# How the last block's results are stored: the first part in column halves, the last part as one 128 KB store per queue

## The chip, the cores and the metric

The kernel runs on one core of one Trainium2 chip. The time is device time in microseconds (us) of one execution; smaller is better. Of the kernel before there are three timed runs (median 608.53 us) and one profiled execution, whose trace all readings below come from.

Engines are named as the profile names them: PE is the matrix engine (its weight loads are PEld), DVE the vector engine, ACT the scalar engine, POOL the general one, SP the engine that mostly issues transfers. A "q" behind a name (SPq, ACTq) means the engine's instruction sequencer, which also issues DMA transfers. DMA transfers are carried out by 16 DMA engines that all queues share.

## The reference

Two stages follow each other. The first is a chunked state-space scan (Mamba-2) over 4 sequences, 8 heads, 768 steps and 32 channels per head, with a state of 16; its output is viewed as 3072 tokens of 256 numbers. The second is a mixture of four experts, all used for every token:

```
p = domain_probs / (domain_probs.sum(-1, keepdims=True) + 1e-09)
for e in range(E):                      # E = 4
    h = np.maximum(x @ w1[e], 0.0)      # (3072, 256) @ (256, 1024)
    out += p[:, e:e + 1] * (h @ w2[e])  # (3072, 1024) @ (1024, 256)
```

Everything is in 32-bit floats. The output is 3072 rows of 256 numbers, 1 KB per row.

## The kernel before, in words

The second stage takes nearly all of the time. The 3072 tokens are 12 pairs of 256 tokens (`NP` = 12), and three pairs form a block (`BLOCKS` = 4). A block is passed over the 16 column blocks of the hidden layer (four experts, four blocks of 256 columns each) in units of four. In each unit the matrix products are done by a fast scheme (`G`): 20 block products in place of 24, paid for by sums and differences on DVE and POOL before and after. The results of the products add up in accumulators, which lie in PSUM banks while PE writes them and otherwise in SBUF tiles called V (`[128, 2, 256]`). At a block's end some 20 additions combine its accumulators into the outputs of the block's three pairs, which the kernel numbers n = 0, 1, 2 and which this text calls parts.

For all blocks but the last this is done under cover of the next block's products (`result`, `leave`). The last block has nothing behind it, so it is ended by a function of its own, `last`. In it each part is turned by PE and copied from PSUM to an SBUF tile whose partition holds tokens and whose free dimensions are s (two sequence halves) and m (the 256 output columns). The work goes by pieces: `piece(d, n, ...)` makes the sum for column half d of part n, lets PE turn both s (two transposes, L1422) and copies the result out (L1435). The pieces come in the order (d=0, n=1), (1, 1), (1, 0), (0, 0), (1, 2). The last piece, column half 0 of part 2, is made differently: its two PSUM banks (`ends`, one for each s, here i) are filled with the turned partial sum, and the last products are added into them (L1498). So the last instruction that computes anything is the copy of s = 1 out of its bank; ACT copies s = 0 and DVE s = 1.

Part n of the block is stored by `send` (L1427). A partition index of the SBUF tile is 64 c + i, with c = 0 or 1, and the output is viewed as follows, so that a step in c is a step of 12 x 64 rows in DRAM:

```
dst = out.rearrange("(s c n i) m -> n c i s m", s=2, c=2, i=HALF)
```

`send` issues one transfer for each c, c = 0 on SP's queue and c = 1 on ACT's, each from 64 partitions. Parts 1 and 0 go as two stores of 128 KB when both column halves are copied; part 2 goes as two stores of 64 KB for each s.

The order of the instructions is not that of the code. Every piece of work is handed to a planner (`Plan.add`), with estimated times for each engine, the values that it reads and writes, and the works that it must follow. `Plan.run` lets all engines advance in planned time. PE's order is fixed beforehand (`line`; `TAILS` puts the transposes among the last products), every other engine takes, of the works that are ready, the one with the earliest due time (`latest`, reckoned back from the end). The engines then get their instructions in the order of planned starts. Three rules of the planner matter here:

```
        for v in part:
            w.needs.update(v.readers)
            v.writers = v.writers + [w]
```

A work that writes a part of a value must follow all works so far that read the value, whatever part of it they read. For a transfer (`kb` set) planned time goes on until its data has landed: it takes `ISSUE` = 0.55 us to issue, 1.4 us more to start, its kilobytes at `RATE` = 330 per us, and 0.7 us. And a work on another engine than SP that follows a transfer is planned `MARGIN` = 2.0 us after the landing.

Of the kernel before, what the change touches and what calls it, by code (L numbers as in the profile page):

```python
# [12 lines left out]
P = 128  # L13
# [7 lines left out]
LANDING = 2.2  # L21
# [9 lines left out]
LANES, ISSUE = 8, .55  # L31
# [328 lines left out]
def kernel(  # L360
# [10 lines left out]
    nc = tc.nc  # L371
# [14 lines left out]
    HALF = P // 2  # L386
# [352 lines left out]
    for x in range(4):  # L739
# [3 lines left out]
        out=a_sb, in_=a.rearrange("c h s -> (c h) s").rearrange("(p r) s -> p r s", r=2))  # L743
    load_w1(1, homes["W"][1])
    nc.sync.dma_start(
        out=homes["gate"][0][:, :2].rearrange("p c s -> p (c s)"),
        in_=p_d[:1, 0].rearrange("x z i -> x (z i)").partition_broadcast(P))
# [38 lines left out]
    for s, copy in enumerate((nc.scalar.copy, nc.vector.tensor_copy)):  # L786
        copy(out=yT0[:, :, P * s:P * s + P].rearrange("p t (c i) -> p c t i", c=2),
             in_=ys[s][:, :FB].rearrange("p (c t i) -> p c t i", c=2, t=NT))
# [7 lines left out]
    for s in range(2):  # L796
        v = bound[HALF * s:HALF * s + HALF]
        nc.gpsimd.affine_select(
            out=v, in_=v, compare_op=ALU.is_ge, fill=0.0, base=0, pattern=[[1, HALF]],
# [4 lines left out]
    plan = Plan(homes)  # L804
# [18 lines left out]
    def value(kind, **kw):  # L823
        return Value(kind, **kw)
# [186 lines left out]
    def flat(v):  # L1011
        return v.t.rearrange("p a m -> p (a m)")
# [12 lines left out]
    def whole(v):  # L1025
        return v.t if v.kind == "bank" else flat(v)
# [298 lines left out]
    def terms_of(key, groups, house, put={}):  # L1325

        return [(acc, weights[key, fbs, 2][0][r],
                 lambda r=r, fbs=fbs: weights[key, fbs, 2][1](r), T[r])
                for acc in house for r in put.get(acc, acc) for fbs, T in groups if r in T]

    def second(k, key, groups, houses, held=(), put={}):

        seq = []
        for house in houses:
            terms = terms_of(key, groups, house, put)
            if terms:
                seq += visit(k, house, terms, house in held)
        return seq
# [9 lines left out]
    def sum_(x, y, sign, o):  # L1348

        vs = dict.fromkeys((x[0], y[0]))  # L1350
        engines = B256 if all(v.kind != "bank" for v in (*vs, o[0])) else {"DVE": D256}
        plan.add(engines, lambda e: (on(e).tensor_add if sign > 0 else on(e).tensor_sub)(  # L1352
            o[1](), x[1](), y[1]()), reads=[v for v in vs if v is not o[0]],
            two=all(v.kind != "bank" for v in vs), writes=[o[0]])

    def accumulators(k, houses):

        def acc(house, i):
            v = kept[k, house]
            return v, lambda: whole(v)[:, i * FB:i * FB + FB]  # L1360

        return {r[0]: acc(h, i) for h in houses for i, r in enumerate(h)}
# [44 lines left out]
    def last(k, groups):  # L1407

        seq = second(k, k, groups, LATE, HELD)
        A = accumulators(k, LATE)  # L1410
        dst = out.rearrange("(s c n i) m -> n c i s m", s=2, c=2, i=HALF)
        tails, last_of = [], (0, 1)

        def fresh():
            v = value("V")
            return v, lambda: v.t[:, 0]

        def into(r, x, y, sign=1):
            sum_(A[x], A[y], sign, A[r])

        def turn(o, t, i, at):
            nc.tensor.transpose(t.t[:, at:at + P], o[1]()[:, i * P:i * P + P], ident)  # L1422

        def send(n, r, to):
            by = ((nc.sync, "SP"), (nc.scalar, "ACT"))
            for c, (queue, on_) in enumerate(by):
                plan.add({on_: ISSUE}, lambda e, c=c, queue=queue: queue.dma_start(  # L1427
                    out=dst[3 * k + n, c][:, to], in_=r.t[HALF * c:HALF * c + HALF, to]),
                    lag=LANDING + .4, kb=64 * (to.stop - to.start), reads=[r], port=False)

        ready = [[value("V")] * 2 for _ in range(2)] + [[value("V") for _ in range(2)]]

        def copied(x, r, t, d, n, to):
            copy = (nc.vector.tensor_copy, nc.scalar.copy)[x]
            plan.add({("DVE", "ACT")[x]: .1 + .13 * (to.stop - to.start)}, lambda e: copy(  # L1435
                out=r.t[:, to, d * P:d * P + P],
                in_=t.t[:, :P * (to.stop - to.start)].rearrange("p (s m) -> p s m", m=P)),
                reads=[t], part=[r])

        def piece(d, n, x, y, sign):  # L1440
            o, rs = fresh(), ready[n]
            ts = [value("bank", fills=False) for _ in dict.fromkeys(rs)]
            sum_(x, y, sign, o)
            tails.append(plan.add({"PE": .35}, lambda e: [
                turn(o, ts[i % len(ts)], i, i * P if len(ts) == 1 else 0) for i in range(2)],
                reads=[o[0]], writes=ts))
            x = len(tails) % 2
            if len(ts) == 1:
                copied(x, rs[0], ts[0], d, n, slice(0, 2))
                if d == last_of[n]:  # L1450
                    send(n, rs[0], slice(0, 2))
            else:
                for i in range(2):
                    copied(0, rs[i], ts[i], d, n, slice(i, i + 1))

        into(9, 9, 10)
        into(7, 7, 9)
        into(7, 7, 15)
        into(15, 15, 13)
        into(9, 9, 11, -1)  # L1460
        into(11, 11, 7, -1)
        q = A["q"] = fresh()
        sum_(A[11], A[13], -1, q)
        into(13, 13, 7)
        into(10, 10, 15)
        into(4, 4, 8)
        into(4, 4, 9)
        into(8, "q", 8, -1)
        into(15, 15, 4)
        piece(0, 1, A[1], A[11], -1)  # L1470
        piece(1, 1, A[5], A[4], 1)
        into(15, 15, 12)
        into(15, 15, 14)
        into(8, 8, 14, -1)
        piece(1, 0, A[16], A[15], -1)
        into(8, 8, 16)
        piece(0, 0, A[0], A[8], 1)

        into(10, 10, 12)
        into(10, 10, 14)  # L1480
        two, three = APART
        terms = terms_of(k, groups, APART)
        begun = kept[k, APART]
        seq += visit(k, APART, terms, True, three)
        third = kept[k, (three,)]
        piece(1, 2, (third, lambda: whole(third)[:, FB:]), A[10], 1)
        o, ends = fresh(), [value("bank", seeded=True) for _ in range(2)]
        sum_((begun, lambda: flat(begun)[:, :FB]), A[13], 1, o)
        tails.extend(plan.add({"PE": .2}, lambda e, t=t, i=i: turn(o, t, i, 0), reads=[o[0]], writes=[t])
                     for i, t in enumerate(ends))  # L1490
        for i, t in enumerate(ends):
            for acc, w, view, x in terms:
                if acc != two:
                    continue

                def fn(e, i=i, t=t, view=view, x=x):
                    for j in range(JJ):
                        nc.tensor.matmul(  # L1498
                            out=t.t[:, :P], lhsT=x.t[:, j, i * P:i * P + P], rhs=view()[:, j],
                            start=False, stop=j == JJ - 1, skip_group_check=True)  # L1500

                seq.append(plan.add({"PE": .52}, fn, reads=[w, x], writes=[t]))
            copied(1 - i, ready[2][i], t, 0, 2, slice(i, i + 1))
            send(2, ready[2][i], slice(i, i + 1))
        return [w for i, x in enumerate(seq)
                for w in (*[t for t, n in zip(tails, TAILS) if n == len(seq) - i], x)]

# [51 lines left out]
    for seq, _ in plain[EARLY:]:  # L1559
# [10 lines left out]
        out=g0.t[:, 2:].rearrange("p c s -> p (c s)"), in_=p_d.rearrange(  # L1570
            "(x a) e z i -> x (a e z i)", x=E)[0, 2 * P:6 * P].partition_broadcast(P)),
        kb=256, reads=[pd], part=[g0])
# [61 lines left out]
    for u, (k, fbs) in enumerate(units):  # L1634
        of_block = [v for v, (q, _) in enumerate(units) if q == k]
        i = u - of_block[0] + (not k)
# [13 lines left out]
        final = u == len(units) - 1  # L1650
        groups = [(fbs, fours_right(h))]
        behind = last(k, groups) if final else second(k, k, groups, G.houses)
        if u == of_block[-1] and k < len(blocks) - 1:
            ending = k, result(k)
# [25 lines left out]
    for w in done:  # L1680
        n = len(traced)
# [52 lines left out]
```

## Time and profile before

| what | value |
|---|---|
| timed runs | 608.45, 608.53, 608.77 us; median 608.53 |
| the profiled execution: own time, span from first to last instruction | 607.16 us, 605.5 us |
| PE busy | 599.2 us, 99% of the span |
| DVE, ACT, POOL busy | 499.6, 277.3, 135.0 us |
| granted clock of PE | 1.000 all through |
| last product and last copy (DVE) end | 601.3 and 601.6 us into the span |
| last store issued, last store landed | 602.0 and 604.25 us into the span |

The page of the profile gives busy times, shares and the costliest groups of instructions; the other views used are the order of time (timeline), who waited for whom, stretches (windows), and the DMA view, which shows in 40 slices of a stretch which share of the 16 DMA engines was busy, in tenths. For single packets and for the steps in which a transfer reports its landing, the records of the trace are used directly: each DMA engine that took part in a transfer reports once, by a write of 4 bytes.

### The profile page before, as it was taken

To read this page: it belongs to the slowest core of one execution; us is meant where nothing else is said; L and a number is where in the kernel's file an instruction comes from. 1 tells how busy PE (TensorE), PEld (TensorE's weight loads), DVE (VectorE), ACT (ScalarE), POOL (GpSimd) and SP (SyncE) were. 2 spreads that over 40 slices of the span, in tenths; PEclk is the share of its full clock that TensorE was granted. 3 is DMA by queue.
4 is the path that set the end of the run, shared out by engine and by line. 5 is a ranking of instruction groups with operands and counts; after the bars stand their busy time and mean duration, and the time that the engine had idled before them with its cause. 6 is when DMAs were issued, how large, how long until landed. Compare 5 with 4: busy or idle time off the path is not lost.

```text
span 605.5 us, 12443 instructions
## 1 busy us (share of the span) xinstructions
PE 599.2 (99%) x4616; PEld 516.3 (85%) x4616; DVE 499.6 (83%) x867; ACT 277.3 (46%) x621; POOL 135.0 (22%) x147
## 2 busy tenths in 40 slices
PE   9999999999999999999999999999999999999997
PEld 6778888888888888888888888888888888888886
DVE  7879999999999995897979988486876989485795
ACT  3456476783443527764242343434444242444530
POOL 7652836656510000465201000000000000000000
PEclk9999999999999999999999999999999999999999
DMA  5786858779625229763422425963242332964001
GB/s 177 222 220 202 252 172 287 222 230 300 219 79 143 55 47 359 232 202 134 139 88 62 144 33 162 291 178 110 87 132 69 97 74 50 364 183 139 0 1 53
DMA packets 100196, 93.98 MB, mean 155 GB/s; under 512 B 34480, under 2 KB 69416, under 8 KB 100136
## 3 DMA queue, kind: packets, MB, share of 16 engines
q1 hardware_dynamic: 99444, 92.70, 50.8%
q8 instruction: 36, 0.59, 0.4%
q10 hardware_dynamic: 628, 0.47, 0.2%
q14 instruction: 24, 0.20, 0.1%
q0 software_dynamic: 64, 0.02, 0.0%
HBM read 72.89 MB, written 20.27 MB: 154 GB/s over the span
## 4 chain that ended last, share of the span: by engine, by line
PE 98%; DVE 2%; ACT 0%; issue 0%
PE bank L1007 91%; PE bank L535 2%; PE bank L502 1%; PE bank L940 1%; PE bank L544 1%; PE bank L690 1%; PE bank L644 1%; DVE v L1053 0%; DVE v L1042 0%; PE bank L1498 0%; DVE MT L510 0%; PE bank L1422 0%; PE bank L659 0%; DVE v L1034 0%; DVE MT L687 0%; ACT v L1052 0%
## 5 line engine op out<-in xcount | busy, mean ns | idle before, releaser
L1007 PE MATMUL bank<-v,w 128*128 128x256 f32 x1876 | 435.3, 380 | 0.8 <-DVE v L1042 0.4
L1007 PEld LDWEIGHTS bank<-v,w 128*128 128x128 f32 x1876 | 354.6, 190 | 52.2 <-DVE v L1042 1.4
L1034 DVE TENSOR_TENSOR v<-v,v 128x512 f32<-128x512 f32 x239 | 176.0, 757 | 3.1 <-ACT v L1016 1.2
L1007 PE MATMUL bank<-Y,w 128*128 128x256 f32 x692 | 177.2, 380 | 0.1
L1316 ACT COPY v<-bank 128x512 f32<-128x512 f32 x120 | 70.3, 586 | 199.5 <-PE bank L1007 199.3
L1007 PEld LDWEIGHTS bank<-Y,w 128*128 128x128 f32 x692 | 130.6, 190 | 19.6 <-ACT v L1016 0.9
L1042 DVE SCALAR_TENSOR_TENSOR v<-bank,gate 128x512 f32<-128x512 f32 x158 | 108.3, 686 | 36.1 <-PE bank L1007 32.4
L1076 POOL TENSOR_TENSOR w<-w,w 128x512 f32<-128x512 f32 (+1 forms) x81 | 90.1, 1122 | 98.0 <-DMA xt<-in_xbc_dram 30.9
L1174 DVE TENSOR_TENSOR bank<-bank,v 128x512 f32<-128x512 f32 x92 | 63.8, 695 | 34.1 <-PE bank L1007 22.9
L1016 ACT COPY v<-bank 128x512 f32<-128x512 f32 x111 | 65.1, 587 | 55.1 <-PE bank L1007 46.2
L1021 ACT COPY bank<-v 128x512 f32<-128x512 f32 x141 | 81.4, 592 | 19.2 <-DVE v L1042 15.6
L518 ACT ACTIVATE MT<-ab,neg 128x64 f32<-128x64 f32 x144 | 37.4, 338 | 0.0
L1034 DVE TENSOR_TENSOR v<-bank,v 128x512 f32<-128x512 f32 x30 | 20.6, 687 | 8.8 <-PE bank L1007 8.2
L1352 DVE TENSOR_TENSOR v<-v,v 128x256 f32<-128x256 f32 x65 | 24.5, 422 | 1.1 <-ACT v L1316 0.9
L902 POOL TENSOR_TENSOR cts<-ctm,dec 128x512 f32<-128x512 f32 x11 | 14.3, 1301 | 40.3 <-DVE v L1034 30.3
L1042 DVE SCALAR_TENSOR_TENSOR v<-v,gate 128x512 f32<-128x512 f32 x30 | 21.6, 719 | 0.4
L959 ACT COPY v<-bank 64x256 f32<-64x256 f32 (+1 forms) x33 | 12.3, 373 | 19.3 <-PE bank L544 16.2
L1034 POOL TENSOR_TENSOR v<-v,v 128x512 f32<-128x512 f32 x11 | 14.0, 1273 | 20.9 <-DVE v L1034 14.0
L687 DVE TENSOR_TENSOR MT<-bank,MT 128x256 f32<-128x256 f32 x47 | 16.7, 415 | 0.2
L523 DVE TENSOR_TENSOR MT<-MT,bound 128x512 f32<-128x512 f32 x18 | 16.0, 895 | 0.7 <-ACT MT L518 0.7
L490 ACT ACTIVATE ctm<-bct,tmask 128x256 f32<-128x256 f32 (+1 forms) x26 | 11.0, 484 | 8.0 <-DMA bct<-in_xbc_dram 4.0
L535 PEld LDWEIGHTS bank<-MT,xt 64*32 64x32 f32 x768 | 9.1, 105 | 2.6 <-issue 1.8
(94 smaller groups left out, 194.0 us busy)
## 6 DMA issues: line engine op xcount, KB each, us to landing
w<-w_d SPq DMA_DIRECT2D x128, 256.0 KB
w<-in_w_dram SPq DMA_DIRECT2D x72, 256.0 KB
w_d<-w SPq DMA_DIRECT2D x64, 256.0 KB
gate<-p_d SPq DMA_DIRECT2D x15, 384.0 KB
xt<-in_xbc_dram SPq DMA_DIRECT2D x48, 96.0 KB
ab<-cum_d SPq DMA_DIRECT2D x36, 128.0 KB
bct<-in_xbc_dram SPq DMA_DIRECT2D x5, 512.0 KB
out_dram<-v SPq DMA_DIRECT2D x144, 16.0 KB
```

The source lines that it names most:

```text
L518: nc.scalar.activation(out=MT[:, q, c, t], in_=ab[:, c, h], func=AF.Exp, bias=neg[:, e, t, i:i + 1])
L535: nc.tensor.matmul(out=y[to:to + 32], lhsT=xt[k, c, h:h + D], rhs=MT[k, q, c, t], start=start, stop=True, tile_position=(HALF * s, to), sk ...
L687: nc.vector.tensor_mul(v, bank[:, FB * half:FB * half + FB], v)
L1007: nc.tensor.matmul(out=o, lhsT=w[:, j], rhs=x if half is None else x[:, j], start=(start and j == 0), stop=(j == 1), skip_group_check=True)
L1016: act(.5, lambda e: nc.scalar.copy(out=flat(v), in_=bank.t), reads=[bank], writes=[v])
L1021: act(.54 if to - lo > FB else .32, lambda e: nc.scalar.copy(out=bank.t[:, lo:to], in_=flat(v)[:, lo:to]), reads=[v], writes=[bank])
L1034: plan.add(engines, lambda e: (on(e).tensor_add if sign > 0 else on(e).tensor_sub)(flat(v), whole(x), whole(y)), reads=[x, y], writes=[v], ...
L1042: dve(D512, lambda e: nc.vector.scalar_tensor_tensor(out=h.t, in0=whole(x).rearrange("p (j m) -> p j m", j=JJ), scalar=0.0, in1=g.t[:, 2 * ...
L1076: (on(e).tensor_add if sign > 0 else on(e).tensor_sub)(out, x, y)
L1174: dve(D512, lambda e: (nc.vector.tensor_add if sign > 0 else nc.vector.tensor_sub)(to.t, bank.t, whole(x)), reads=[x, bank], writes=[to])
L1316: act(.5, lambda e: nc.scalar.copy(out=flat(v), in_=bank.t), reads=[bank], writes=[v], hold=HOLD)
L1352: plan.add(engines, lambda e: (on(e).tensor_add if sign > 0 else on(e).tensor_sub)(o[1](), x[1](), y[1]()), reads=[v for v in vs if v is n ...
```

## The change

Two things change in `last`.

Part 0 is stored by column halves: after the piece (1, 0), its column half d = 1 is sent (two stores of 64 KB, one on each queue, 128 runs of 512 bytes each), and after the piece (0, 0) the half d = 0 in the same way. Part 1 goes as before.

Part 2 is stored by `send_half`: for each s, one store of 128 KB from all 128 partitions, s = 0 on SP's queue and s = 1 on ACT's. The DRAM side of this store has the sizes (c, i, m) = (2, 64, 256), the SBUF side (128, 256). The number of store instructions stays eight, four on each queue.

```diff
-        def send(n, r, to):
-            by = ((nc.sync, "SP"), (nc.scalar, "ACT"))
-            for c, (queue, on_) in enumerate(by):
-                plan.add({on_: ISSUE}, lambda e, c=c, queue=queue: queue.dma_start(
-                    out=dst[3 * k + n, c][:, to], in_=r.t[HALF * c:HALF * c + HALF, to]),
-                    lag=LANDING + .4, kb=64 * (to.stop - to.start), reads=[r], port=False)
+        queues = {"SP": nc.sync, "ACT": nc.scalar}
+
+        def send(n, r, ds=slice(0, 2)):
+            m, size = slice(P * ds.start, P * ds.stop), ds.stop - ds.start
+            for c, on_ in enumerate(queues):
+                plan.add({on_: ISSUE}, lambda e, c=c, on_=on_: queues[on_].dma_start(
+                    out=dst[3 * k + n, c][:, :, m], in_=r.t[HALF * c:HALF * c + HALF, :, m]),
+                    lag=LANDING + .4, kb=64 * size, reads=[r], port=False)
+
+        def send_half(n, r, i, on_):
+            plan.add({on_: ISSUE}, lambda e: queues[on_].dma_start(
+                out=dst[3 * k + n][:, :, i], in_=r.t[:, i]),
+                lag=LANDING + .4, kb=128, reads=[r], port=False)
...
                 copied(x, rs[0], ts[0], d, n, slice(0, 2))
-                if d == last_of[n]:
-                    send(n, rs[0], slice(0, 2))
+                if n == 0:
+                    send(n, rs[0], slice(d, d + 1))
+                elif d == last_of[n]:
+                    send(n, rs[0])
...
             copied(1 - i, ready[2][i], t, 0, 2, slice(i, i + 1))
-            send(2, ready[2][i], slice(i, i + 1))
+            send_half(2, ready[2][i], i, ("SP", "ACT")[i])
```

## The prediction

> **What bounds the kernel now.** First the page: busy times and the chain that ended last.
>
> ```profile
> span 605.5 us, 12443 instructions
> PE 599.2 (99%) x4616; PEld 516.3 (85%) x4616; DVE 499.6 (83%) x867; ACT 277.3 (46%) x621; POOL 135.0 (22%) x147
> ...
> PE 98%; DVE 2%; ACT 0%; issue 0%
> ```
>
> PE fills the span up to about 601.3. The change touches nothing that PE waits for, so only the few microseconds behind PE can move. The order of time over the end shows them (start, duration, engine, line, what):
>
> ```profile
> 598.87 0.37 ACT L1435 COPY v<-bank 128x256 f32<-128x256 f32 x1 [3.47 <-PE bank L1422]
> 599.84 0.98 DVE L1435 COPY v<-bank 128x256 f32<-128x256 f32 x3 [0.64 <-PE bank L1422]
> 600.22 0.27 ACT L1435 COPY v<-bank 128x128 f32<-128x128 f32 x1 [0.97 <-PE bank L1498]
> 600.24 1.06 PE L1498 MATMUL bank<-w,v 128*128 128x128 f32 x8
> 600.29 2.29 ACTq L1427 DMA_DIRECT2D out_dram<-v  x3
> 601.33 0.29 DVE L1435 COPY v<-bank 128x128 f32<-128x128 f32 x1 [0.51 <-PE bank L1498]
> ```
>
> ACT's copy at 598.87 is piece (1, 0). DVE's three from 599.84 are piece (0, 0), 128x256, and the two of piece (1, 2), 128x128, at 600.33 and 600.53. The last copy (s = 1) ends at 601.62. After that there are only stores: SP issues its last at 601.75; ACT its own at 601.96, because its issue before (601.05, 0.81 us) has only just ended. Then the waits of SP, with total, times and longest:
>
> ```profile
> SPq L1730 <- DMA out_dram<-v: 1.9, 1, 1.9
> ```
>
> SP closes the program once all stores have landed: the last report of a landing is at 604.25, the span ends 1.25 later. Issue to last landing is 2.33 us on SP (604.08) and 2.29 on ACT. Last, the DMA view, once from 601 to 605.5 and once from 173.9 to 176.4, where little but the loads of `ah` (128 partitions of 256 bytes each) runs:
>
> ```profile
> DMA  0000049899979999987699840000000000000000
> ...
> DMA  0155620000015552000001666300000134432910
> ...
> ah<-cumh_d SPq DMA_DIRECT2D x2, 32.0 KB
> ```
>
> The closing stores use nine tenths of the 16 DMA engines, though they are small. An `ah` load alone, between idle slices, stays at five to six tenths, or eight engines; its packet records hold 8 completion writes of 4 bytes where a closing store's hold 16. Its SBUF side has 128 partitions, its DRAM side is (8, 16, 64). The start of the kernel has two more such rows: loads whose slowest dimension is 4 report landings from 4 engines, stores of 24 partitions from 12. All of these fit one reading: the engines are as many as divide the slowest dimension of both sides, 16 at most.
>
> **The change, part by part.**
>
> *Part 2 as one store per queue.* It takes two of the four last stores away. What that saves: ACT's last issue need not wait for another one, so it starts at 601.70 in place of 601.96 (-0.2 us). But the new store's DRAM side is (2, 64, 256): its slowest dimension is c, whose step is 12 x 64 rows, so that it can't be merged with i. By the reading above 2 engines carry it, 64 packets of 1 KB each, where a 64 KB store now gives 4 packets to each of 16. No row shows two engines; the price of a packet is there: 46 ns is the median of all 6,264 packets of 1 KB, and the 16 packets that an `ah` load gives each engine run back to back (16 x 18 = 0.29 us of a burst of 0.30 to 0.39). So 64 x 46 = 2.94 us for one store alone.
>
> SP's store (s = 0) needs the copies that end at 600.49 and 600.62; its queue is free, so it issues at about 600.70. From issue to a first packet it takes 1.29 (600.29 to 601.58) to 1.34 us: 602.0. ACT's store (s = 1) issues at 601.70, first packet 603.05; SP's is then a third through. Do they share the two engines? Bounds: apart, ACT's ends at 603.05 + 2.94 = 606.0 at the earliest; on the same two, 128 packets take 5.89 from 602.0, to 607.9. I take the same two: over the 36 `ah` loads after 23 us, issued four in a row, more than 12 packets overlap for 0.05 us in all, where 2 KB loads on 16 engines overlap up to 21; if each load took the next eight engines, overlapping loads would fill 16. That row is of one queue only, so both ends stay.
>
> The Trainium skill, page "DMA: Bandwidth & Descriptors", section "Why a DMA increments its semaphore by 16 and not by 1", says that such a transfer gets the largest count up to 16 that divides the slowest dimension of both sides, and on SP's and ACT's queues the lowest-numbered engines. By that rule both stores sit on the same two engines, and the sum is the one for 607.9; the trace agrees on the count (8, 4, 12), and no run here shows which engines.
>
> *Part 0 in halves.* One more issue on each queue. The half d = 1 is ready at 599.24, issues at 599.30 on both and is through by 599.95 (0.64), at worst 600.11 (0.81): before ACT's copy at 600.22, so this costs nothing; without that cover ACT's copy, and SP's store behind it, would be late by the excess. Its packets (512 bytes, 27 ns median, 8 per engine per store) come at 600.6 to 601.6, before part 2's. The half d = 0 does not go earlier. In the planner its copy writes part of the value that the first half's stores read, so it must follow them: they land 0.55 + 1.4 + 2 x 64/330 + 0.7 = 3.04 us after the copy of (1, 0), plus a margin of 2.0. From 599.24 that is 604.3 in the trace's time, and the last copy is planned for 601.33. So DVE's order turns round: the two copies of (1, 2), the last copy, then the copy of (0, 0), 128x256, 0.42 us, from about 601.6 to 602.05. Nothing is queued behind it on DVE, and its bank is wanted by none. If the program also makes it wait for the landing of the half d = 1 (599.30 + 2.54 to 2.90, by the 128 KB stores at 600.29), it runs to 602.2 to 602.65. Its two stores then issue last: SP at 602.1, and ACT behind its part 2 store at 602.4 (up to 602.7). On 14 engines they land by about 605; on the pair they add 2 x 8 x 27 ns = 0.43 us.
>
> *Due times.* Sums for piece (1, 0) become due about 2 us sooner, which may swap additions on DVE between 586 and 599. DVE idles 0.66 us before 593.03 and 0.37 before 596.93 waiting for PE, and PE's order is fixed: 0, bounds -0.3 to +0.3.
>
> *Sum.* Pair busy from 602.0 for 5.89 + 0.43: 608.3. Last packet to last landing is now 0.35 to 0.54 (599.13 to 599.48, 603.71 to 604.25): 608.75 in place of 604.25, +4.5 us. The span becomes 610.0 against 605.5, the profiled execution 611.7 against its own 607.16 (1.66 outside the span). The median stands 1.37 above that execution; the difference added to it gives 613.0.
>
> The packet's price may be higher with two queues on one engine: in 601 to 605 SP's packets have a mean of 63.3 ns and ACT's 50.4, and SP's at 597.9, with ACT's behind them, 79.5. At the mean of the first two, 57, the pair takes 1.4 more (614.4), at 79 4.2 more (617.2). Such a packet's time may hold waiting beside the other queue's packet on the same engine, while the engine moves data all along; so I stay with 46.
>
> **The rivals.**
>
> *Two pairs of engines* (both queues pick differently): SP's done by 605.2, ACT's by 606.4 with the halves, landed 606.9: +2.6, 611.1. For it: no row of two queues. Against: the `ah` row.
>
> *Sixteen engines after all* (not slower than can be told): the store is spread as by its 128 partitions. Then 128 KB give 8 packets per engine and only the turned order counts. ACT's store of the half d = 0 issues at 602.4 to 602.7 and lands 2.3 to 2.5 later: 604.7 to 605.2, +0.45 to +0.95, so 609.0 to 609.5. It decides from the point where an engine gets so few packets that the half d = 0 lands last: with four engines part 2 still ends at 605.8 (64 x 46 ns = 2.94 from 602.0, 0.43, 0.4), with eight it does not. Against it: `ah` has the same 128 partitions and got 8.
>
> *The change does what it says*: sixteen engines and the copy of (0, 0) in its old place. Part 1's two stores, issued together at 596.58, landed at 599.15 and 599.48, so a second half-store trails by 0.33; with one store fewer behind each other the end comes near 604.1: 608.4. The Trainium skill, same page, section "Rules for kernel authors", advises exactly this: one 128-partition transfer in place of two on partition halves, since these share the engines; the trace agrees that they trail each other (0.33 us). By that rule alone the time would be 608.4. Against: the count of engines, and the planner's rule.
>
> **How the numbers follow.** A measurement of this kernel can tell some 0.2% (1.2 us) from no change: under 607.3 is faster, over 609.75 slower. Chances: same pair at 46 to 57 ns, 0.67 (612.7 to 614.4, its own range); same pair and dearer packets, 0.08 (to 617.2); two pairs, 0.13 (611.1); sixteen engines with turned order, 0.09; as it says, 0.02; faster for a reason I don't see, 0.01. Slower therefore 0.88, same 0.11, faster 0.01. The range takes the first and third whole and half of the second: 610.6 to 615.8.
>
> **What would show it.** In the DMA view after 602, a long stretch at one tenth where now nine tenths stand for two microseconds; landing reports of part 2's stores from 2 engines; SP's closing wait near 6 us. DVE's last copy of L1435 is 128x256, after the 128x128 ones, and its stores are issued last on both queues. PE's last matmul ends at 601.3 within 0.3. The prediction is wrong if part 2's stores report from 16 engines, if packets on the pair take far from 46 ns, or if PE's end moves.

## The result, and the profile after

The changed kernel takes 613.54 us (median of 6 runs, 612.09 to 614.54) against 608.49 us (6 runs, 607.74 to 608.77): a ratio of 1.0087, 95% interval 1.0074 to 1.0101. That is 5.05 us more; forecast were 4.5, 613.0 us.

The profiled execution has a span of 612.0 us. Its page:

```profile
span 612.0 us, 12443 instructions
PE 599.0 (98%) x4616; PEld 515.8 (84%) x4616; DVE 502.2 (82%) x867; ACT 277.5 (45%) x621; POOL 134.3 (22%) x147
```

PE has the same work and its share is lower: something was added around it. The order of time over the end (start, duration, engine, line, what; PE's rows left out):

```profile
600.85 0.64 ACTq L1429 DMA_DIRECT2D out_dram<-v  x1
601.80 0.27 ACT L1442 COPY v<-bank 128x128 f32<-128x128 f32 x1 [0.98 <-PE bank L1507]
601.91 0.49 DVE L1442 COPY v<-bank 128x128 f32<-128x128 f32 x2 [1.13 <-PE bank L1422]
602.27 0.58 SPq L1434 DMA_DIRECT2D out_dram<-v  x1
602.91 0.62 DVE L1442 COPY v<-bank 128x128 f32<-128x128 f32 x2 [0.51 <-PE bank L1507]
603.24 0.59 ACTq L1434 DMA_DIRECT2D out_dram<-v  x1
603.57 0.62 SPq L1429 DMA_DIRECT2D out_dram<-v  x1
603.93 0.61 ACTq L1429 DMA_DIRECT2D out_dram<-v  x1
```

The copy of s = 1, the last one that waits for a product of PE, starts at 602.91 where it started at 601.33. The row at 602.91 holds two copies: the second, from 603.12, is the 128x256 one of piece (0, 0), which was the first of DVE's copies before. Its two stores are the last to be issued. Behind them SP waits for 6.5 us:

```profile
SPq L1739 <- DMA out_dram<-v: 6.5, 1, 6.5
```

The DMA view of the stretch from 602.9 to the end (slices of 0.23 us) shows what for:

```profile
DMA  0001111122023468941111110111111110000000
```

Before, the closing stores filled nine tenths of the DMA engines for two microseconds. Now there is one short peak, with some two microseconds at one or two tenths ahead of it and three and a half at one tenth behind it. The landing records say who works there: each of part 2's stores reports from two engines, s = 0 at 4.35 us after the start of the copy of s = 1, s = 1 at 7.74. The last of all is ACT's store of part 0's half d = 0: fourteen of its reports come by 4.6, the last two only at 7.94 and 7.95, when the two engines of s = 1 are free. These two engines are called the **pair** below, as in the prediction.

A measure that leaves the rest of the kernel out is used from here on, the **tail**: from the start of DVE's copy of s = 1 to the end of the span. It was 4.13 us (601.33 to 605.46, the span unrounded; 4.17 in the expectations below, from the rounded one) and is 9.09, so +4.96. What is left of the difference between the two profiled spans, 1.59 us, is upstream: PE is 1.06 us late at 14 us into the span, 0.70 at 20 and 1.47 by 33, and stays within 0.3 of that to the end. On DVE, ACT, POOL and SP both kernels have the same instructions in the same order up to this end; PE's records differ from each other only in the order of some small products and weight loads, nearly all in the first 11 us, as they do between the runs below too. This lateness comes and goes from run to run: PE's last matmul ended between 601.1 and 603.5 us in the profiled executions below, 601.1 in one with the changed kernel's order. It is hardly in the medians: the execution profiled before was 1.33 us under its median, the one after 0.18 over its own.

### The profile page after: what moved, and what is told of

It is laid out like the page before. It is cut to its first block, busy times and chain, and to the rows that moved or that the text cites. A ratio compares the mean times of both kernels' runs of the same rounds, so it can differ in the third digit from the quotient of the medians.

```text
span 612.0 us, 12443 instructions
## 1 busy us (share of the span) xinstructions
PE 599.0 (98%) x4616; PEld 515.8 (84%) x4616; DVE 502.2 (82%) x867; ACT 277.5 (45%) x621; POOL 134.3 (22%) x147
## 4 chain that ended last, share of the span: by engine, by line
PE 94%; DVE 2%; DMA 1%; issue 1%; SPq 0%; ACT 0%; DVEq 0%; POOL 0%; POOLq 0%
PE bank L1007 90%; PE bank L535 1%; PE bank L940 1%; PE bank L502 1%; DMA w<-in_w_dram 1%; DVE v L1042 1%; PE bank L544 1%; DMA v<-in_a_dram 0%; PE bank L1507 0%; SPq L471 0%; DVE MT L523 0%; PE bank L1422 0%; DVE v L1034 0%; DVE MT L687 0%; DVE MT L510 0%
```

## The experiments

### Part 2 stored as before

Part 2 goes back to its four stores of 64 KB, called **quarters** from here on:

```diff
         def send_half(n, r, i, on_):
-            plan.add({on_: ISSUE}, lambda e: queues[on_].dma_start(
-                out=dst[3 * k + n][:, :, i], in_=r.t[:, i]),
-                lag=LANDING + .4, kb=128, reads=[r], port=False)
+            for c, on_ in enumerate(queues):
+                plan.add({on_: ISSUE}, lambda e, c=c, on_=on_: queues[on_].dma_start(
+                    out=dst[3 * k + n, c][:, i], in_=r.t[HALF * c:HALF * c + HALF, i]),
+                    lag=LANDING + .4, kb=64, reads=[r], port=False)
```

> The changed kernel with part 2 stored as before (four stores of 64 KB), part 0 still in column halves. The measure is the tail: from the start of DVE's copy of s = 1 (128x128, the last one that PE's products wait on) to the end of the span; 4.17 us before (601.33 to 605.5), 9.09 after the change (602.91 to 612.0). Theory 1 (two engines carry part 2's stores): the tail falls to 4.6 to 5.1, what is left over 4.17 being the turned order (copy of (0, 0) last); time 609.0 to 609.5. Rival 2 (the turned order and the half stores of part 0 cost the time): the tail stays at 8.5 to 9.1, time 613.

Measured: 608.86 us against 608.11, ratio 1.0015 (1.0004 to 1.0026); tail 4.85. The tail is as theory 1 had it; the time is 0.14 us under its range, and the kernel before took 0.38 less in these runs than in those above. The DVE order is still turned:

```profile
602.41 0.62 DVE L1443 COPY v<-bank 128x128 f32<-128x128 f32 x2 [0.52 <-PE bank L1508]
```

So taking part 2's stores back removes 4.24 of the 4.96 us, and the rest of the change by itself costs 0.72.

### Part 0 stored whole

```diff
-                if n == 0:
-                    send(n, rs[0], slice(d, d + 1))
-                elif d == last_of[n]:
+                if d == last_of[n]:
                     send(n, rs[0])
```

> The changed kernel with part 0 stored whole as before, part 2 still as one 128 KB store per queue. Theory 1 (two engines): nearly all of the loss stays; the pair carries 128 packets of 1 KB at 46 to 54 ns and no 512-byte ones, so the tail is 7.9 to 8.9, time 612.3 to 613.3. Rival 2 (turned order, halves): tail back at 4.2, time 608.5. Rival 3 (the halves of part 0 block the pair beside part 2's stores): tail 6.5 to 7.5.

Measured: 613.4 us, ratio 1.0087 (1.007 to 1.0103); tail 9.60. Theory 1 named the cause, but its size was wrong: without the halves and the turned order the tail is not shorter but 0.51 longer, so the two parts of the change do not simply add up. Two things differ in the records. SP's store of s = 0 is issued 0.29 us before the start of the last copy instead of 0.65, since the whole store of part 0 stands ahead of it on the queue; and the pair still carries its share of part 0's packets then, whose last reports come 1.50 (SP) and 2.01 us (ACT) after that start. One of the two engines reports 0.86 us after the other for both of part 2's stores (5.23 and 6.09, 7.56 and 8.42), where they report together after the change. Why one lags was not settled.

### Part 0's halves in two tiles

On top of the first experiment, so that the planner has no reader of the tile ahead of the second copy:

```diff
+        apart = [value("V") for _ in range(2)]
...
-                copied(x, rs[0], ts[0], d, n, slice(0, 2))
+                r = apart[d] if n == 0 else rs[0]
+                copied(x, r, ts[0], d, n, slice(0, 2))
                 if n == 0:
-                    send(n, rs[0], slice(d, d + 1))
+                    send(n, r, slice(d, d + 1))
```

> As the run with part 2 stored as before, but the two column halves of part 0 lie in two tiles, so that the planner sees no reader of the first half ahead of the second copy. Theory: the copy of (0, 0) goes back before those of (1, 2) on DVE and the tail is 4.0 to 4.3, time 608.3 to 608.6: the turned order was all that the first half of the change cost. Rival: the half stores of part 0 cost something by themselves (two more issues, 512-byte packets): tail 4.5 to 5.0.

Measured: 607.56 us, ratio 0.9993 (0.9983 to 1.0003); tail 3.80. DVE's order is the old one:

```profile
601.50 0.98 DVE L1445 COPY v<-bank 128x256 f32<-128x256 f32 x3 [0.64 <-PE bank L1422]
602.99 0.29 DVE L1445 COPY v<-bank 128x128 f32<-128x128 f32 x1 [0.51 <-PE bank L1511]
```

The order alone is 4.85 - 3.80 = 1.05 us. The halves without it save 0.33 of the tail against before, which puts it 0.2 under the range expected; the time can't tell that from nothing.

### The number of engines, with nothing else changed

Part 2's two stores keep their size, source and queue and go to a DRAM tensor aside, whose slowest dimension is A = 2, 4 or 8 with gaps, or 128 rows in one piece (there the tile is 128 x 256 and written whole). These kernels leave part 2's rows of the output unwritten:

```diff
+        aside = [tc.dram_tile([A, 2, 128 // A, 2 * P], FP32, name=f"aside{i}") for i in range(2)]
...
-                out=dst[3 * k + n][:, :, i], in_=r.t[:, i]),
+                out=aside[i][:, 0], in_=r.t[:, i]),
```

> The changed kernel, but part 2's two stores of 128 KB go to a DRAM tensor aside, so that its 704 of 768 output rows per quarter stay as they are and part 2's are left unwritten. The DRAM side is (2, 64, 256) with a gap between the two, as in the output: a control. Theory 1 (the engine count is what divides the slowest dimension of both sides): tail 8.8 to 9.3 as after the change (9.09), landing reports from 2 engines. Rival 2 (something of the output tensor's rows, or DRAM pages 768 KB apart): the tail falls clearly, below 8.

> The same with a DRAM side of (4, 32, 256) with gaps; part 2's output rows are left unwritten. Theory 1: reports from 4 engines; 2 x 32 packets of 1 KB each and the halves' 16 of 512 bytes, from 0.6 us after the copy's start at 46 to 55 ns: 3.0 to 3.9 us; tail 5.2 to 6.2. Rival 2 (one 128-partition store on the DRAM side of several pieces is slow whatever their number): 9.

> The same with a DRAM side of (8, 16, 256) with gaps; part 2's output rows are left unwritten. Theory 1: reports from 8 engines, 2 x 16 packets each, 1.5 to 2.2 us; the turned order decides now: tail 4.6 to 5.2. Rival 2: 9.

> The same with a DRAM side of 128 rows in one piece; part 2's output rows are left unwritten. Theory 1: reports from 16 engines, tail 4.5 to 5.1, that is the price of the turned order alone, 0.4 to 0.9 over before. Rival 2: 9.

Measured, in us; landings count from the start of the copy of s = 1. These four kernels, and the four below them, ran once each:

| slowest dimension in DRAM | engines that report | s = 0 landed | s = 1 landed | part 0's last half landed | tail |
|---|---|---|---|---|---|
| 2 | 2 | 4.35 | 7.81 | 8.01 | 9.15 |
| 4 | 4 | 2.70 | 6.25 | 6.46 | 7.60 |
| 8 | 8 | 1.98 | 4.07 | 4.44 | 5.58 |
| 128 | 16 | 1.04 | 2.04 | 3.67 | 4.81 |

The closing wait of SP in the runs with 2, 4 and 8:

```profile
SPq L1741 <- DMA aside<-v: 6.5, 1, 6.5
```

```profile
SPq L1741 <- DMA aside<-v: 5.0, 1, 5.0
```

```profile
SPq L1741 <- DMA aside<-v: 2.8, 1, 2.8
```

The control (2) repeats the changed kernel's tail (9.15 for 9.09), so neither the output's rows nor their distance matter; with 16 engines only the turned order is left, as in the first experiment (4.81 for 4.85). These two agreements also show how well a tail repeats. The engine count is therefore shown as the cause. The middle cases came out dearer than expected (7.60 for 5.2 to 6.2, 5.58 for 4.6 to 5.2). With four engines s = 0 took 1.79 us for its 32 packets per engine, 56 ns each, near the price; s = 1 took 3.59 for as many, with part 0's half stores among them.

### One queue, one store

Both of part 2's stores on SP:

```diff
-            send_half(2, ready[2][i], i, ("SP", "ACT")[i])
+            send_half(2, ready[2][i], i, "SP")
```

> The changed kernel with both of part 2's 128 KB stores on SP's queue. After the change ACT's first packet of 1 KB came only when SP's 64 per engine were out. Theory A (the two stores share one pair and are served one after the other whatever the queue): reports from two engines, the second store's packets begin within 0.1 us of the first one's end, tail 8.7 to 9.5. Rival B (the pair loses time by changing between two queues): without the change between queues the pair needs some 1 us less, tail 7.8 to 8.4. Rival C (SP's and ACT's stores had different pairs, and waited for something else): the tail grows beyond 10.

Measured: tail 9.07; reports from two engines at 4.37 and 7.50 to 7.74. The packet counts by half microseconds are those of the two queues to within a few, so changing between queues is not what costs; that nothing changes also fits one pair for both queues.

Then s = 1 alone as such a store, with s = 0 in quarters (`send_quarters` issues them as `send_half` does in the first experiment) and part 0 in two tiles as above:

```diff
-            send_half(2, ready[2][i], i, ("SP", "ACT")[i])
+            if i:
+                send_half(2, ready[2][i], i, "ACT")
+            else:
+                send_quarters(2, ready[2][i], i)
```

> Part 0's halves in two tiles, s = 0 of part 2 as two 64 KB stores as before, s = 1 alone as one 128 KB store on ACT: the price of one such store with nothing beside it. Theory 1 with the prediction's price: issued 0.32 after the start of the copy, first packet 1.2 later, 64 packets at 46 to 54 ns = 2.9 to 3.4 us, 0.35 to land, 1.2 to the end: tail 6.0 to 6.6. Rival (a two-engine store costs much more than its packets): above 7.

Measured: tail 6.59. The store is issued late, because ACT's issue of a quarter before it took 0.88 us:

```profile
601.11 0.88 ACTq L1440 DMA_DIRECT2D out_dram<-v  x1
602.09 0.59 ACTq L1434 DMA_DIRECT2D out_dram<-v  x1
```

It lands 4.82 us after its issue, where the last two quarters before the change took 2.3. From 2.0 us after the start of the copy, in steps of half a microsecond, 18, 17, 17, 18, 24, 22 and 8 of its packets start (124 of 128; the first four lie among the quarters'). 23 to 24 in half a microsecond, the most that the pair reaches in these runs, is one packet in 43 ns on each engine; a fresh store stays below that for two microseconds and then reaches it.

The other way round, s = 0 as one store on SP and s = 1 in quarters, part 0 whole, was to show whether a queue holds up the other:

> Part 0 whole, of part 2 s = 0 as one 128 KB store on SP (two engines), s = 1 as two 64 KB stores, one on each queue (16 engines). Theory A (a transfer comes to the engines only after the descriptors of the one before it are handed out, also across the queues): the first landing reports of ACT's 64 KB store come only when s = 0's packets are nearly out, 3.5 to 4.5 us after the start of the copy of s = 1; tail 5.8 to 6.4. Rival B (queues don't hold each other up): ACT's store reports from 14 engines about 2.5 to 2.9 us after that copy's start as before the change, and only the pair is late; tail 5.4 to 6.2.

Measured: tail 6.97, above both. ACT's quarter, on all 16 engines, first reports 3.18 us after the start of the copy, 2.86 after its issue, where the same store before the change needed 1.86. That is between the two theories: it is held up by about 1 us, but not until s = 0 is out (4.85 and 5.60). The changed kernel has the same: ACT's half store of part 0 first reports 3.04 us after its issue, and 2.16 in the kernel with part 2 as before. The series of engine counts has it too: this half store first reports 3.04, 2.96, 1.97 and 2.05 us after its issue where part 2's stores run on 2, 4, 8 and 16 engines. That a store on two engines delays later ones on other engines is shown, and by the run here also on another queue; by what, is open.

### The change without its side effects

Two tiles for part 0, and part 2's stores to 128 rows aside:

> Both parts of the change without their two side effects: the column halves of part 0 in two tiles (no turned order), part 2's two 128 KB stores to 128 rows in one piece of a DRAM tensor aside (16 engines; part 2's output rows are left unwritten). The tail was 4.13 us before, 3.80 with two tiles and four stores of 64 KB. Theory 1: one store per queue that all engines carry saves a little more, since ACT issues the last one right behind the copy (0.32 us after its start) and it lands 1.4 to 2.3 us later: tail 3.1 to 3.8. Rival: the second stores on the queues were worth nothing (16 engines are kept busy either way): 3.8 to 4.2.

Measured: tail 3.40, 0.73 under before. ACT issues its store in 0.34 us, right behind the copy:

```profile
602.63 0.34 ACTq L1436 DMA_DIRECT2D aside<-v  x1
```

So one store per queue would have been worth 0.40 us over the two-tile kernel, if its rows lay together in the output. They do not; that kernel leaves them out of it.

## Why the prediction was right

The time lies 0.5 us from the forecast, and by the predicted mechanism. Step by step, with the times from the start of the copy of s = 1:

- **Two engines for part 2's stores**: right, confirmed by their landing reports and by the series of engine counts. What had shown it beforehand was the `ah` loads, with 128 partitions on one side and 8 on the other.
- **The same two for both queues**: right as far as the records tell, which do not name the engines. ACT's first packet of 1 KB came at 3.98, SP's last ended at 4.01, and one queue gives the same tail. Of the two bounds (packets out at 606.0 or 607.9) the row of `ah` pointed to the right one. The Trainium skill's rule, page "DMA: Bandwidth & Descriptors", section "Why a DMA increments its semaphore by 16 and not by 1", holds here in its count (2, 4, 8, 16) and, as far as the order of the packets tells, in that two stores get the same engines; which ones, by number, no run here shows.
- **The packet's price** was mis-sized. The pair was busy for 7.04 us (603.49 to 610.53), predicted 6.32. A single packet still took 46 ns (median, both stores), but 64 of them took 3.44 us in each store, one in 54 ns: s = 0 ran below the full rate for its first two microseconds, s = 1 lost time while SP's half store of part 0 was on the pair. The trace before had means of 50.4 and 63.3 ns, which the prediction set aside as waiting; here the slower pace was real.
- **The sum** came out closer than its largest term, by luck in part: the pair's 0.72 us too little was made up by 0.29 too much in three others (first packet 0.58 after the start of the copy for 0.67, last packet to last landing 0.34 for 0.43, from there to the end of the span 1.14 for 1.25). The tail is 9.09, forecast 8.67.
- **First packets, issues**: s = 0 issued at -0.65 (predicted -0.63), first packet 1.22 later (1.3); s = 1 at 0.32 (0.37).
- **The turned order**: right, and priced right with the halves: +0.72 in the first experiment, +0.45 to +0.95 predicted. The order alone is 1.05. The copy of (0, 0) followed the last one at once, so it did not wait for the landing of the half d = 1: it started at 603.12 us into the span, and that half's last report came at 603.22.
- **Part 0's half d = 1 costs nothing**: right; its issue on ACT was through at 601.49, and the copy came at 601.80. That the halves are a gain, 0.33 us of the tail with the old order and, together with the turned order, 0.51 beside part 2's stores on two engines, was not seen.
- **Half d = 0 on the other 14 engines by about 605**, which is 3.7 after the copy: they reported at 3.9 to 4.5, since their packets were held up.
- **PE's end within 0.3 us** failed in the profile (602.88 for 601.3), though the prediction had named it as a sign of being wrong. The cause is the variation at the start told above, not the due times: DVE's order up to the end is unchanged.
- The rival "sixteen engines, turned order" would have been 609.0 to 609.5; the kernel with part 2 as before, which comes near that case, took 608.86 against 608.11, +0.75 where +0.45 to +0.95 was worked out, and the run with part 2's stores to 128 rows aside, which is that case but for where the data goes, has a tail 0.68 over before. The gain of the rival "as it says" was put too low: 3.40 for the tail is 0.73 less than before, not 0.1. The advice of the Trainium skill, page "DMA: Bandwidth & Descriptors", section "Rules for kernel authors", one 128-partition transfer in place of two on partition halves, holds where the DRAM side is one piece (0.40 us here) and turns into a loss of 4.24 us where its slowest dimension is 2.

## What to carry to other kernels

Before two transfers are merged into one, look at the slowest dimension of both sides: a store from 128 partitions whose DRAM side starts with a 2 ran on two engines here, and the trace shows it in the number of landing reports and in a long stretch at one tenth. Price such a store by its packets on one engine, add those of every other transfer that uses these engines, and expect other transfers to be late too. Where a planner or a dependency tracker goes by whole tiles, a store of the first half stands ahead of the copy of the second half; two tiles remove that.

## What the runs showed that was not expected

- A store of 128 KB from 128 partitions to 128 rows in one piece can be issued in 0.32 us; its first packet then comes 0.82 us after the issue starts, and it has landed after 1.69 (beside other stores 0.53 and 2.13). The quarters, 64 partitions to 64 rows, took 0.49 to 0.9 us to issue and, with no two-engine store in the way, 1.95 to 2.8 to land.
- Packets of two queues did not take turns on the pair: s = 1 was issued at 0.32 and, with the 1.22 us that s = 0 needed, would have had its first packet at 1.5; it came at 3.98, when s = 0 was out. The trace before shows the like on 16 engines: of part 1's two stores, issued together, SP's packets run from 597.92 to 598.79 and ACT's from 598.62 to 599.13. Packets of a third store, in 512-byte pieces, did come between those of s = 1.
- A fresh two-engine store runs at some two thirds of the rate that the same engines reach two microseconds later (13 to 18 packets in half a microsecond, then 22 to 24).
